# A fused attention and MoE kernel: all attention in native float32, in runs of whole batches between whole blocks of the first MoE product

## The chip, the cores and the metric

The kernel runs on one core of one Trainium2 chip. The metric is device time in microseconds (us), lower is better. PE is TensorE (its weight loads are listed apart as PEld), ACT is ScalarE, DVE is VectorE, POOL is GpSimd, SP is SyncE, which issues the DMAs.

## What is computed

```python
# q, k, v: (8 batches, 12 heads, 448 tokens, 64), float32
scores = scale * q @ k.T - log(448)
attn   = 1 / (1 + exp(-scores))          # a sigmoid, no softmax: no sum over a row
x      = (attn @ v)                      # -> (8*448 tokens, 12*64 = 768)
h      = x @ w_in                        # (3584, 768) @ (768, 2048)
g      = h * clip(h + 3, 0, 6) / 6
out    = g @ w_out                       # (3584, 2048) @ (2048, 768)
```

`w_in` and `w_out` arrive as float64 and are put together on the chip into two float32r parts, high and low.

## The kernel before, in words

**Precision.** A product of float32 accuracy is made in one of two ways. Either both operands are split into a high and a low float32r part and three matmuls are added up (high by high, high by low, low by high), or one matmul is given float32 operands as they are ("native"). A native matmul shows as two records in the trace.

**Attention, native (batches 0 to 2, lines 213 to 259).** Two heads make a pair, 6 pairs a batch. A step takes one chunk of 128 keys for both heads of a pair: two score matmuls on 64 of the 128 rows of the array each (L229), one sigmoid of 128x896 on ACT (L231), two matmuls with v that fill 64 of the 128 columns each (L248). The 64 keys left over (448 = 3 x 128 + 64) of two pairs make one step of quarter tiles, 64x64, the tail (L227, L246). Two pairs are 7 steps, three batches 63 steps. The steps go in groups of two: two steps' scores, then the v products of the group before. Score tiles `sc` have 2 buffers of two PSUM banks. The result of a pair (`pv`) is copied as a high part by ACT (L258) and a low part by DVE (L259) into the blocks `x` that the first MoE product reads.

**Attention, float32r (batches 3 to 7, lines 162 to 211 and 261 to 341).** q, k and v of a pair are split by ACT, DVE and POOL (`prep`), scores take 4 matmuls per chunk (L274, L275) and 3 for the tail (L271), the v products 4 (L331) and 3 (L318). Each chunk has two sigmoids and a subtraction (L279 to L281). After each chunk's scores, 12 matmuls of the first MoE product are put in, up to the end of the last batch: 48 of them and 30 attention matmuls make one pair.

**First MoE product (`moe_in(t)`, L379).** 7 token tiles of 512; each has 16 blocks of 18 matmuls, 288 in all. A block ends in an ACT and a DVE instruction (L383, L384) and a DMA of `g` to DRAM. Its PSUM tile `ph` has 2 buffers. `moe_in(0)` follows the native attention; what is left of the 32 units of w_in (`load_wi`: a DMA, 7 operations on ACT, DVE and POOL, a split) is put together beside it, the first 22 units during the native attention. `moe_in(6)` follows the last attention, and w_out is put together beside it.

**Second MoE product (L543).** 2016 matmuls to the end, beside them reads of `g` and their splits.

**What sets the order.** During batches 0 to 2 and `moe_in(0)` the order on PE, ACT, DVE and POOL is that of the program text; after that only PE's order is. `feed` calls the three parts of a w_in unit (load; join; split) at fixed groups. Each engine works through its own list in order.

Of the kernel before, what the change touches and what calls it, by code (L numbers as in the profile page):

```python
# [20 lines left out]
NST = NC + 1  # L21
# [9 lines left out]
PA = NB * NP  # L31
SB = PA * NST
PEND = 3 * S - 2 * T
LN = 2 * NC
NSN = PA // 2 * (LN + 1)
KB = 3
KM = 12
KU = 14
NSL = 4
NWP = 15  # L40
NWA = 22
NPL = 160
NPP = 224
# [63 lines left out]
def tile_kernel(ctx: ExitStack, tc: tile.TileContext, qk, vP, wi, wo, outT):  # L107
# [33 lines left out]


    zero = att.tile([P, D], F32, tag="x", name="zero", bufs=1)
    nc.gpsimd.memset(zero, 0.0)
    blk = [{n: att.tile([P, P], F32R, tag=f"{n}{u}", name=f"{n}_{u}", bufs=1) for n in ("kbh", "kbl", "vbh", "vbl")} for u in range(2)]

    raw, ops = {}, {}
    qp = []

    def load_native(p):  # L150
        b, hp = divmod(p, NP)
        t = att.tile([P, 2, S], F32, tag=("ka", "ka", "a", "kn")[p % 4], name=f"qkn_{p}", bufs=(2, 2, 1, 1)[p % 4])
        v = att.tile([P, 2 * NC + 1, D], F32, tag=("vv", "vv", "qp0", "qp1")[p % 4], name=f"vn_{p}", bufs=(2, 2, 1, 1)[p % 4])
# [9 lines left out]
    def load(p):  # L163
        b, hp = divmod(p, NP)
        t = att.tile([P, 2, 2, S], F32, tag="qkr", name=f"qkr_{p}", bufs=1)
        v = att.tile([P, 2 * NC + 1, D], F32, tag="vr", name=f"vr_{p}", bufs=1)
        for u in (1, 0):
            for own in halves:
                nc.sync.dma_start(out=t[own, u], in_=qk[b, hp, :, u].rearrange("(j d) s -> d j s", j=2))
        nc.sync.dma_start(out=v, in_=vP[b, hp])  # L170
        raw[p] = t[:, 0], t[:, 1], v

    def prep(p):
        qr, kr, vr = raw.pop(p)
        bk = blk[p % 2]
        qh = att.tile([P, 2, S], F32R, tag="qh", name=f"qh_{p}")
        ql = att.tile([P, 2, S], F32R, tag="ql", name=f"ql_{p}")
        ka = att.tile([P, 2, S], F32R, tag="ka", name=f"ka_{p}")
        nc.vector.tensor_copy(ka, kr)
        for j in range(2):  # L180
            other = halves[1 - j]
            nc.gpsimd.tensor_tensor(  # L182
                out=ka[other, j], in0=kr[other, j], in1=ka.bitcast(F32)[other, j], op=ALU.subtract
            )
        nc.scalar.copy(qh, qr)  # L185
        nc.vector.tensor_tensor(out=ql, in0=qr, in1=qh.bitcast(F32), op=ALU.subtract)  # L186
        vv = att.tile([P, 2, NC, P], F32R, tag="vv", name=f"vv_{p}")
        for j in range(2):
            own, other = halves[j], halves[1 - j]
            vj, vb = vr[:, j * NC : (j + 1) * NC], vr[own, 2 * NC]  # L190
            nc.vector.tensor_copy(vv[:, j, :, own], vj)
            nc.gpsimd.tensor_tensor(  # L192
                out=vv[:, j, :, other], in0=vj, in1=vv.bitcast(F32)[:, j, :, own], op=ALU.subtract
            )
            nc.vector.tensor_copy(bk["vbh"][own, own], vb)
            nc.gpsimd.tensor_tensor(
                out=bk["vbl"][own, own], in0=vb, in1=bk["vbh"].bitcast(F32)[own, own], op=ALU.subtract
            )
        ops[p] = qh, ql, ka, vv

    def prep_block(p):
        qh, ql, ka, _ = ops[p]
        bk = blk[p % 2]
        qp[:] = [att.tile([P, S], F32R, tag=f"qp{u}", name=f"qp{u}_{p}", bufs=1) for u in range(2)]
        for j in range(2):
            own, other = halves[j], halves[1 - j]
            nc.vector.tensor_copy(bk["kbh"][own, own], ka.bitcast(F32)[own, j, NC * P :])
            nc.vector.tensor_copy(bk["kbl"][own, own], ka.bitcast(F32)[other, j, NC * P :])
            nc.vector.tensor_copy(qp[0][own], qh.bitcast(F32)[own, j])
            nc.vector.tensor_copy(qp[1][own], ql.bitcast(F32)[own, j])  # L210

    at = {}

    def native(n):

        m, r = divmod(n, LN + 1)
        return ((2 * m, 2 * m + 1), None) if r == LN else ((2 * m + r // NC,), r % NC)

    def scores_native(n):
        ps, c = native(n)  # L220
        sc = ps_s.tile([P, 2, 512], F32, tag="sc", name=f"scn_{n}")
# [12 lines left out]
    def av_native(n):  # L234
        ps, c = native(n)
        a = at.pop(n)
        for u, p in enumerate(ps):
            v = ops[p][2]
            if c == 0:
                odd = p // 2 % 2  # L240
                pv[p] = (ps_m if odd else ps_a).tile([P, 512], F32, tag="ph" if odd else f"pv{p % 2}", name=f"pv_{p}")
            for j in range(2):
                out = pv[p][halves[j], :S]
                if c is None:
                    rows = halves[j if u == 0 else 1 - j]
                    nc.tensor.matmul(out, v[rows, 2 * NC], a[rows, u], start=False, stop=True)  # L246
                else:
                    nc.tensor.matmul(out, v[:, j * NC + c], a[:, j], start=(c == 0), stop=False)  # L248
        for p in ps if c is None else ():
            b, hp = divmod(p, NP)  # L250
            pt = pv.pop(p)
            for u, (t, c0, q0, n) in enumerate(pieces(b)):
                if u and b == NB - 1:
                    hold(b)
                    nc.vector.tensor_copy(pend[b][:, hp, :n], pt[:, q0 : q0 + n])
                    continue
                xh, xl = (x[:, c0 : c0 + n] for x in block(t, hp))
                nc.scalar.copy(xh, pt[:, q0 : q0 + n])  # L258
                nc.vector.tensor_tensor(out=xl, in0=pt[:, q0 : q0 + n], in1=xh.bitcast(F32), op=ALU.subtract)  # L259

    def scores(s):
        p, c = divmod(s, NST)
        sc = ps_s.tile([P, 2, 512], F32, tag="sc", name=f"sc_{s}")
        last = c == NC
        cs = slice(c * P, min((c + 1) * P, S))
        js = slice(0, 1 if last else 2)
        qh, ql, ka, _ = ops[p]
        if last:
            kbh, kbl = blk[p % 2]["kbh"], blk[p % 2]["kbl"]
            for n, (k_, q_) in enumerate(((kbh, qp[0]), (kbh, qp[1]), (kbl, qp[0]))):  # L270
                nc.tensor.matmul(sc[:, 0, :S], k_, q_, start=(n == 0), stop=(n == 2))  # L271
        else:
            for j in range(2):
                nc.tensor.matmul(sc[:, j, :S], ka[:, j, cs], qh[:, j], start=True, stop=False)  # L274
                nc.tensor.matmul(sc[:, j, :S], ka[:, j, cs], ql[:, j], start=False, stop=True)  # L275
        ah = att.tile([P, 2, S], F32R, tag="ah", name=f"ah_{s}")
        al = att.tile([P, 2, S], F32R, tag="al", name=f"al_{s}")
        a = att.tile([P, 2, S], F32, tag="a", name=f"a_{s}", bufs=1)
        nc.scalar.activation(ah[:, js], sc[:, js, :S], AF.Sigmoid, bias=bias_s, scale=scale)  # L279
        nc.scalar.activation(a[:, js], sc[:, js, :S], AF.Sigmoid, bias=bias_s, scale=scale)  # L280
        nc.vector.tensor_tensor(out=al[:, js], in0=a[:, js], in1=ah.bitcast(F32)[:, js], op=ALU.subtract)  # L281
        at[s] = sc, ah, al

    pv, xf, xb, pend = {}, {}, {}, {}

    def block(t, cc):
# [4 lines left out]
        return xb[t, cc]  # L291

    def hold(b):
        if b not in pend:
            pend[b] = xpl.tile([P, NCC, PEND], F32, tag="pend", name=f"pend_{b}")

    def flush(b):

        t, c0, _, n = pieces(b)[1]
        for cc in range(NCC):  # L300
            xh, xl = (x[:, c0 : c0 + n] for x in block(t, cc))
            x = pend[b][:, cc, :n]
            nc.vector.tensor_copy(xh, x)
# [139 lines left out]
    for s in range(SB, NSTEP + 1):  # L443
# [10 lines left out]
        if s % BS == 1:  # L454
            for _ in moe:
                pass
# [133 lines left out]
```

## Time and profile before

| | |
|---|---|
| median of 3 runs | 1224.88 us (1224.79 to 1225.37) |
| the profiled execution | 1225.24 us, of which the span in the trace 1223.2 us |
| first matmul starts at | 4.15 us |
| native attention (batches 0 to 2) ends at | 116.0 us |
| last attention (batch 7) ends at | 695.1 us |
| second MoE product starts at | 762.4 us |

A row of the trace gives a start or a count, then a duration; what stands behind an arrow (`<-`) ended the idle time before an instruction. The chain is the work that ended last, followed back from the last instruction. Times of merged matmuls include the gaps of their pipeline.

### The profile page before, as it was taken

Reading aid. Unit: us, or ns where it says so; the run is one execution under the profiler, and the core shown is the slowest. Engines: PE = TensorE matmul, PEld = TensorE weight load, DVE = VectorE, ACT = ScalarE, POOL = GpSimd, SP = SyncE. Lnnn points to the kernel's source line nnn. Section 1 sums busy time; section 2 is a strip of 40 time slices with the busy share of each in tenths; the row PEclk is TensorE's granted clock in tenths of the full one; section 3 lists DMA queues with packets and bytes.
Section 4 is the critical chain, followed back from the end, with each engine's and each line's share of the span. In section 5 each row is a group of like instructions: output and inputs, shape, how many; then the busy total and the mean of one; then the engine's idle time right before and its main releaser. Section 6 shows DMA issues by size and latency. Waiting matters only on the chain.

```text
span 1223.2 us, 15074 instructions
## 1 busy us (share of the span) xinstructions
PE 1212.2 (99%) x5508; PEld 960.8 (79%) x5508; DVE 727.2 (59%) x1284; ACT 519.9 (43%) x671; POOL 256.8 (21%) x297
## 2 busy tenths in 40 slices
PE   8999999999999999999999999999999999999998
PEld 2334788888888888888888888888888888888887
DVE  4566868889889888888987598972030303030300
ACT  6776335666666666666656444331010202020200
POOL 3344452333333433434333100000000000000000
PEclk9999999999999999999999999999999999999999
DMA  7644544443334433343432368624040404040000
GB/s 252 195 154 126 162 129 120 118 119 111 105 94 120 118 111 100 99 119 111 118 96 66 93 206 295 232 91 159 26 163 18 164 26 163 27 155 26 26 26 26
DMA packets 62570, 142.68 MB, mean 117 GB/s; under 512 B 8224, under 2 KB 29728, under 8 KB 58912
## 3 DMA queue, kind: packets, MB, share of 16 engines
q1 hardware_dynamic: 62496, 141.72, 36.7%
q8 instruction: 43, 0.70, 0.2%
q14 instruction: 31, 0.25, 0.1%
HBM read 101.32 MB, written 40.37 MB: 116 GB/s over the span
## 4 chain that ended last, share of the span: by engine, by line
PE 95%; DVE 2%; ACT 1%; DMA 1%; issue 1%; POOL 0%; SPq 0%; DVEq 0%; POOLq 0%; ACTq 0%
PE po L543 37%; PE ph L379 36%; PE pv L331 6%; PE scn L229 3%; PE sc L274 3%; PE sc L275 3%; PE pv L248 3%; PE sc L318 1%; PE sc L271 1%; ACT an L231 1%; DMA qkn<-qk 1%; PE scn L227 1%; PE pv L246 0%; DMA qkr<-qk 0%; DVE wiql L60 0%
## 5 line engine op out<-in xcount | busy, mean ns | idle before, releaser
L379 PE MATMUL ph<-x,wi 128*128 128x512 f32 x2016 | 485.7, 391 | 2.4 <-DVE g L384 2.4
L379 PEld LDWEIGHTS ph<-x,wi 128*128 128x128 f32 x2016 | 378.0, 188 | 79.0 <-DVE g L384 4.4
L543 PE MATMUL po<-gh,woh 128*128 128x512 f32 x672 | 261.4, 389 | 0.0
L543 PE MATMUL po<-gl,woh 128*128 128x512 f32 x672 | 261.4, 389 | 0.0
L543 PE MATMUL po<-gh,wol 128*128 128x512 f32 x672 | 261.4, 389 | 0.0
L550 DVE TENSOR_SCALAR o<-po 128x512 f32<-128x512 f32 x42 | 29.0, 690 | 294.1 <-PE po L543 294.1
L503 ACT CAST gh<-gr 128x2048 fp32r<-128x2048 f32 x28 | 53.6, 1914 | 298.1 <-PE po L543 294.0
L281 DVE TENSOR_TENSOR al<-a,ah 128x896 fp32r<-128x896 f32 x120 | 141.3, 1177 | 48.6 <-ACT a L280 47.6
L543 PEld LDWEIGHTS po<-gh,woh 128*128 128x128 f32 x672 | 126.1, 188 | 26.3
L543 PEld LDWEIGHTS po<-gl,woh 128*128 128x128 f32 x672 | 126.1, 188 | 26.2
L543 PEld LDWEIGHTS po<-gh,wol 128*128 128x128 f32 x672 | 126.1, 188 | 26.1
L279 ACT ACTIVATE ah<-sc,bias_s 128x896 fp32r<-128x896 f32 x120 | 110.0, 917 | 73.5 <-PE sc L275 38.0
L182 POOL TENSOR_TENSOR ka<-qkr,ka 64x448 fp32r<-64x448 f32 x60 | 91.7, 1529 | 124.2 <-issue 111.1
L280 ACT ACTIVATE a<-sc,bias_s 128x896 f32<-128x896 f32 x120 | 109.2, 910 | 2.5 <-DVE al L281 1.0
L383 ACT ACTIVATE g<-ph,bias 128x512 f32<-128x512 f32 x112 | 77.1, 688 | 69.0 <-PE ph L379 59.9
L384 DVE SCALAR_TENSOR_TENSOR g<-g,ph 128x512 f32<-128x512 f32 x112 | 76.2, 681 | 18.0 <-ACT g L383 17.7
L504 DVE TENSOR_TENSOR gl<-gr,gh 128x2048 fp32r<-128x2048 f32 x28 | 64.1, 2289 | 29.1 <-ACT gh L503 29.0
L231 ACT ACTIVATE an<-scn,bias_s 128x896 f32<-128x896 f32 x63 | 60.4, 1007 | 23.3 <-PE scn L229 18.4
L274 PE MATMUL sc<-qh,ka 128*128 128x448 f32 x180 | 65.8, 366 | 0.0
L275 PE MATMUL sc<-ql,ka 128*128 128x448 f32 x180 | 65.7, 365 | 0.0
L192 POOL TENSOR_TENSOR vv<-vr,vv 128x192 fp32r<-128x192 f32 x60 | 35.3, 609 | 143.7 <-issue 141.2
L186 DVE TENSOR_TENSOR ql<-qkr,qh 128x896 fp32r<-128x896 f32 x30 | 57.3, 1910 | 5.3 <-ACT qh L185 3.2
(84 smaller groups left out, 1154.4 us busy)
## 6 DMA issues: line engine op xcount, KB each, us to landing
gd<-g SPq DMA_DIRECT2D x112, 256.0 KB, 2.9
gr<-gd SPq DMA_DIRECT2D x28, 1024.0 KB, 5.4
qkr<-qk SPq DMA_DIRECT2D x120, 224.0 KB, 3.9
ws<-wo SPq DMA_DIRECT2D x24, 512.0 KB, 4.9
outT<-o SPq DMA_DIRECT2D x42, 256.0 KB, 2.0
qkn<-qk SPq DMA_DIRECT2D x18, 448.0 KB, 4.6
wiqh<-wi SPq DMA_DIRECT2D x20, 384.0 KB, 3.5
vr<-vP SPq DMA_DIRECT2D x30, 224.0 KB, 2.6
```

Of the source, the lines that this page charges most:

```text
L182: nc.gpsimd.tensor_tensor(out=ka[other, j], in0=kr[other, j], in1=ka.bitcast(F32)[other, j], op=ALU.subtract)
L231: nc.scalar.activation(a, sc[:, :, :S], AF.Sigmoid, bias=bias_s, scale=scale)
L274: nc.tensor.matmul(sc[:, j, :S], ka[:, j, cs], qh[:, j], start=True, stop=False)
L275: nc.tensor.matmul(sc[:, j, :S], ka[:, j, cs], ql[:, j], start=False, stop=True)
L279: nc.scalar.activation(ah[:, js], sc[:, js, :S], AF.Sigmoid, bias=bias_s, scale=scale)
L280: nc.scalar.activation(a[:, js], sc[:, js, :S], AF.Sigmoid, bias=bias_s, scale=scale)
L281: nc.vector.tensor_tensor(out=al[:, js], in0=a[:, js], in1=ah.bitcast(F32)[:, js], op=ALU.subtract)
L331: nc.tensor.matmul(pv[p][j][:, :S], vv[:, j, c, :], a_[:, j], start=(c == 0 and a_ is ah), stop=(c == NC - 1 and a_ is al),)
L379: nc.tensor.matmul(ph, w[:, cc], x, start=(n == 0), stop=(n == 3 * NCC - 1))
L383: i1 = nc.scalar.activation(g, ph, AF.Relu, bias=bias_3, scale=1.0)
L384: i2 = nc.vector.scalar_tensor_tensor(out=g, in0=g, scalar=6.0, in1=ph, op0=ALU.min, op1=ALU.mult)
L543: nc.tensor.matmul(po[t, ec], w[:, fc], x[:, u], start=(fc == 0 and n == 0), stop=(fc == NFC - 1 and n == 2))
```

## The change

All eight batches take the native path; `load` (with its copies), `prep`, `prep_block`, the float32r `scores` and `av` are removed with their splits, second sigmoids and subtractions. Steps go in groups of three (`GS = 3`): the scores of three steps, then the v products of the three steps before. The tail of two pairs is now the fourth of their 7 steps, not the seventh. A batch is a run by itself (21 steps, 7 groups); batches 0 to 2 are one run of 63 steps. Between the runs stand whole `moe_in` blocks with no attention in them: run(0 to 2), `moe_in(0)`, `moe_in(1)`, run(3), `moe_in(2)`, run(4), `moe_in(3)`, run(5), `moe_in(4)`, run(6), `moe_in(5)`, run(7), then `moe_in(6)` as before. The score tiles have 3 buffers (6 PSUM banks), which `ph` of `moe_in(0)` to `moe_in(5)` uses too; `pv` has one buffer for even and one for odd pairs; `moe_in(6)` has 4 buffers. 20 units of w_in, not 22, are put together during the first run, one a group but for one group; the other 12 beside `moe_in(0)`, the last one issued at matmul 238 of 288. The order of all four engines is that of the text up to the end of the last attention.

```diff
-NSL = 4
-NWA = 22
+LC = 2 * NC + 1
+LB = NP // 2 * LC
+GS = 3
+NWA = 20
...
-    ps_m = ph1.enter_context(tc.tile_pool(name="ps_m", bufs=2, space=bass.MemoryType.PSUM, side="right"))
-    att = ph2.enter_context(tc.tile_pool(name="att", bufs=2))
-    ps_s = ph2.enter_context(tc.tile_pool(name="ps_s", bufs=2, space=bass.MemoryType.PSUM))
+    att = ph2.enter_context(tc.tile_pool(name="att", bufs=1))
+    ps_s = ph2.enter_context(tc.tile_pool(name="ps_s", bufs=GS, space=bass.MemoryType.PSUM))
...
+        t = att.tile([P, 2, S], F32, tag="qk", name=f"qk_{p}", bufs=4)
+        v = att.tile([P, 2 * NC + 1, D], F32, tag="v", name=f"v_{p}", bufs=4)
...
+    def step(n):
+        m, r = divmod(n, LC)
+        return ((2 * m, 2 * m + 1), None) if r == NC else ((2 * m + (r > NC),), r % (NC + 1))
...
-        a = att.tile([P, 2, S], F32, tag=("ah", "al")[n % 2], name=f"an_{n}")
+        a = att.tile([P, 2, S], F32, tag="a", name=f"a_{n}", bufs=2 * GS)
...
+        sa = att.tile([P, 4 * w], I32, tag="wis", name=f"wis_{n}", bufs=4)
...
-            ph = (ps_x if t == NT - 1 and fc % 2 else ps_m).tile([P, T], F32, tag="ph", name=f"ph_{t}_{fc}")
+            if t < NT - 1:
+                ph = ps_s.tile([P, 2, T], F32, tag="sc", name=f"ph_{t}_{fc}")[:, 0]
+            else:
+                ph = ps_m.tile([P, T], F32, tag="ph", name=f"ph_{t}_{fc}")
...
+    def attention(first, last, w_in=False):
+        for s in range(first, last, GS):
+            i = (s - first) // GS
+            if w_in:
+                feed(0, i)
+                if s == 0:
+                    load(1)
+                feed(1, i)
+            for n in range(s, s + GS):
+                scores(n)
+            if w_in:
+                feed(2, i)
+            for n in range(s - GS, s):
+                if n >= first:
+                    av(n)
+            for n in range(s, s + GS):
+                m, r = divmod(n, LC)
+                if r in (0, NC) and (p := 2 * m + 2 + (r == NC)) < B * NP:
+                    load(p)
+        for n in range(last - GS, last):
+            av(n)
...
+        attention(0, NB * LB, True)
+        for n, _ in enumerate(moe_in(0)):
+            i, r = divmod(n, KU)
+            if r == 0:
+                for part in range(3):
+                    feed(part, NG0 + i)
+        for n, _ in enumerate(moe_in(1)):
+            if n % (3 * NCC) == 0 and n // (3 * NCC) < NCC:
+                flush(NB - 1, n // (3 * NCC))
+        for b in range(NB, B):
+            attention(b * LB, (b + 1) * LB)
+            if b < B - 1:
+                for _ in moe_in(b - 1):
+                    pass
```

## Rows read from the trace of the kernel before

**Rows 1.** Page, busy time of each engine (share of the span) and its instructions.

```profile
PE 1212.2 (99%) x5508; PEld 960.8 (79%) x5508; DVE 727.2 (59%) x1284; ACT 519.9 (43%) x671; POOL 256.8 (21%) x297
```

**Rows 2.** Waits of PE, all: total us, times, longest us.

```profile
PE scn L229 <- DMA qkn<-qk: 4.2, 1, 4.2
PE ph L379 <- DVE g L384: 2.4, 3, 1.3
PE scn L229 <- ACT an L231: 0.6, 2, 0.3
```

**Rows 3.** Chain in order of time, native attention: start us, us, what; two records a matmul.

```profile
26.30 0.91 PE scn L227 x8
27.22 1.65 PE pv L248 x8
28.87 1.70 PE scn L229 x8
30.57 0.90 PE pv L248 x4
31.48 0.91 PE pv L246 x8
...
40.02 0.95 PE scn L229 x4
...
50.46 0.91 PE scn L227 x8
```

**Rows 4.** Chain, batches 3 to 7 and the MoE products behind them.

```profile
672.57 0.61 PE sc L271 x3
...
684.45 0.81 PE pv L331 x4
...
689.63 0.61 PE sc L271 x3
...
695.09 67.36 PE ph L379 x297
762.45 456.97 PE po L543 x2016
```

**Rows 5.** Chain at the start of the native attention.

```profile
4.15 5.79 PE scn L229 x16
9.94 1.65 PE pv L248 x8
11.60 1.70 PE scn L229 x8
13.30 1.65 PE pv L248 x8
14.96 0.91 PE scn L227 x8
```

**Rows 6.** Timeline of PE, end of the native attention: start us, us, what.

```profile
116.01 8.46 PE L379 MATMUL ph<-x,wi 128*128 128x512 f32 x36
125.05 49.74 PE L379 MATMUL ph<-x,wi 128*128 128x512 f32 x216 [0.58 <-DVE g L384]
```

**Rows 7.** Chain, two places in the native attention where PE waits for a sigmoid.

```profile
59.25 0.91 ACT an L231
...
60.21 1.92 PE scn L229 x8
...
83.37 0.56 ACT wis L58
83.92 0.91 ACT an L231
...
84.87 1.92 PE scn L229 x8
```

**Rows 8.** ACT by line and shape, 4 to 116 us: count, busy us, mean ns, idle before.

```profile
L231 ACT ACTIVATE an<-scn,bias_s 128x896 f32<-128x896 f32 x63 | 60.4, 1007 | 23.3 <-PE scn L229 18.4 <-PE scn L227 4.6
```

**Rows 9.** Stretch 60 to 90: PE, PEld, DVE, ACT, POOL busy us, granted clock, DMA.

```profile
60.00:90.00 30.00, 29.50 (x156) 9.20 (x156) 20.49 (x42) 23.82 (x39) 11.62 (x12) 1.00 0.46 145
```

More of the change, by code (lines that the diff above doesn't have):

```diff
@@ L20 @@
 NC = S // P
-NST = NC + 1
 NP = H // 2
@@ L30 @@
 NB = 3
-PA = NB * NP
-SB = PA * NST
 PEND = 3 * S - 2 * T
[L34 to L37, printed above, removed]
+LC = 2 * NC + 1
+LB = NP // 2 * LC
+GS = 3
 KU = 14
-NSL = 4
-NWP = 15
-NWA = 22
-NPL = 160
-NPP = 224
+NWA = 20
 NWU = 1.4
@@ L140, in tile_kernel, with load @@
     nc.scalar.activation(warm, bias_s, AF.Sigmoid)
[L143 to L150, printed above, removed]
+    ops, at, pv, xb, pend = {}, {}, {}, {}, {}
+    def load(p):
         b, hp = divmod(p, NP)
-        t = att.tile([P, 2, S], F32, tag=("ka", "ka", "a", "kn")[p % 4], name=f"qkn_{p}", bufs=(2, 2, 1, 1)[p % 4])
-        v = att.tile([P, 2 * NC + 1, D], F32, tag=("vv", "vv", "qp0", "qp1")[p % 4], name=f"vn_{p}", bufs=(2, 2, 1, 1)[p % 4])
+        t = att.tile([P, 2, S], F32, tag="qk", name=f"qk_{p}", bufs=4)
+        v = att.tile([P, 2 * NC + 1, D], F32, tag="v", name=f"v_{p}", bufs=4)
         nc.sync.dma_start(out=t, in_=qk[b, hp])
@@ L161, in load_native @@
         ops[p] = t[:, 0], t[:, 1], v
[L163 to L221, printed above, removed]
+    def step(n):
+        m, r = divmod(n, LC)
+        return ((2 * m, 2 * m + 1), None) if r == NC else ((2 * m + (r > NC),), r % (NC + 1))
+    def scores(n):
+        ps, c = step(n)
+        sc = ps_s.tile([P, 2, 512], F32, tag="sc", name=f"sc_{n}")
@@ L229, in scores_native @@
                     nc.tensor.matmul(sc[:, j, :S], k[halves[j], c * P : (c + 1) * P], q[halves[j]], start=True, stop=True)
-        a = att.tile([P, 2, S], F32, tag=("ah", "al")[n % 2], name=f"an_{n}")
+        a = att.tile([P, 2, S], F32, tag="a", name=f"a_{n}", bufs=2 * GS)
         nc.scalar.activation(a, sc[:, :, :S], AF.Sigmoid, bias=bias_s, scale=scale)
         at[n] = a
[L234 to L282, printed above, removed]
@@ L284, in tile_kernel @@
-    pv, xf, xb, pend = {}, {}, {}, {}
     def block(t, cc):
@@ L291, in block, with flush @@
         return xb[t, cc]
[L293 to L297, printed above, removed]
+    def flush(b, cc):
         t, c0, _, n = pieces(b)[1]
[L300 to L303, printed above, removed]
-            nc.vector.tensor_tensor(out=xl, in0=x, in1=xh.bitcast(F32), op=ALU.subtract)
-    def av(s):
-        p, c = divmod(s, NST)
-        b, hp = divmod(p, NP)
-        last = c == NC
-        vv = ops[p][3]
-        if c == 0:
-            pv[p] = [ps_a.tile([P, 512], F32, tag=f"pv{u}", name=f"pv{u}_{p}") for u in range(2)]
-        sc, ah, al = at.pop(s)
-        if last:
-            vbh, vbl = blk[p % 2]["vbh"], blk[p % 2]["vbl"]
-            out = sc[:, 1, :S]
-            for n, (v_, a_) in enumerate(((vbh, ah), (vbl, ah), (vbh, al))):
-                nc.tensor.matmul(out, v_, a_[:, 0], start=(n == 0), stop=(n == 2))
-            x = xf.pop(p)
-            (t, c0, q0, n), *rest = pieces(b)
-            nc.vector.tensor_tensor(out=x[:, :n], in0=out[:, :n], in1=x[:, :n], op=ALU.add)
-            xh, xl = (x_[:, c0 : c0 + n] for x_ in block(t, hp))
-            nc.vector.tensor_copy(xh, x[:, :n])
-            nc.gpsimd.tensor_tensor(out=xl, in0=x[:, :n], in1=xh.bitcast(F32), op=ALU.subtract)
-            for _, _, q0, n in rest:
-                hold(b)
-                nc.vector.tensor_tensor(out=pend[b][:, hp, :n], in0=out[:, q0 : q0 + n], in1=x[:, q0 : q0 + n], op=ALU.add)
-            return
-        for a_ in (ah, al):
-            for j in range(2):
-                nc.tensor.matmul(
-                    pv[p][j][:, :S], vv[:, j, c, :], a_[:, j],
-                    start=(c == 0 and a_ is ah), stop=(c == NC - 1 and a_ is al),
-                )
-        if c == NC - 1:
-            pt = pv.pop(p)
-            x = xf[p] = att.tile([P, S], F32, tag="x", name=f"x_{p}", bufs=1)
-            for j in range(2):
-                own, other = halves[j], halves[1 - j]
-                nc.scalar.copy(x[own], pt[j][other, :S])
-                nc.vector.tensor_tensor(out=x[own], in0=pt[j][own, :S], in1=x[own], op=ALU.add)
@@ new lines, in flush, with av @@
+        xh, xl = (x[:, c0 : c0 + n] for x in block(t, cc))
+        x = pend[b][:, cc, :n]
+        nc.vector.tensor_copy(xh, x)
+        nc.vector.tensor_tensor(out=xl, in0=x, in1=xh.bitcast(F32), op=ALU.subtract)
+    def av(n):
+        ps, c = step(n)
+        a = at.pop(n)
+        for u, p in enumerate(ps):
+            v = ops[p][2]
+            if p not in pv:
+                pv[p] = ps_a.tile([P, 512], F32, tag=f"pv{p % 2}", name=f"pv_{p}")
+            for j in range(2):
+                out = pv[p][halves[j], :S]
+                if c is None:
+                    rows = halves[j if u == 0 else 1 - j]
+                    nc.tensor.matmul(out, v[rows, 2 * NC], a[rows, u], start=(u == 1), stop=(u == 0))
+                else:
+                    nc.tensor.matmul(
+                        out, v[:, j * NC + c], a[:, j],
+                        start=(p % 2 == 0 and c == 0), stop=(p % 2 == 1 and c == NC - 1),
+                    )
+        p = ps[0]
+        if c is None or (p % 2 and c == NC - 1):
+            b, hp = divmod(p, NP)
+            pt = pv[p]
+            for u, (t, c0, q0, w) in enumerate(pieces(b)):
+                if u and b == NB - 1:
+                    if b not in pend:
+                        pend[b] = xpl.tile([P, NCC, PEND], F32, tag="pend", name=f"pend_{b}")
+                    nc.vector.tensor_copy(pend[b][:, hp, :w], pt[:, q0 : q0 + w])
+                    continue
+                xh, xl = (x[:, c0 : c0 + w] for x in block(t, hp))
+                nc.scalar.copy(xh, pt[:, q0 : q0 + w])
+                nc.vector.tensor_tensor(out=xl, in0=pt[:, q0 : q0 + w], in1=xh.bitcast(F32), op=ALU.subtract)
@@ L355, in load_wi @@
         hi, lo = (w_[fc][:, cs].rearrange("p c f -> p (c f)") for w_ in (wih, wil))
-        own = n % NSL if n < NWP else n % (NSL - 1)
-        if own == 2:
-            sa = att.tile([P, 4 * w], I32, tag="qkr", name=f"wis_{n}", bufs=1)
-            st, ab = sa[:, : 2 * w], sa[:, 2 * w :]
-        elif own == 3:
-            sa = xpl.tile([P, 4 * w], I32, tag="pend", name=f"wis_{n}")
-            st, ab = sa[:, : 2 * w], sa[:, 2 * w :]
-        else:
-            st, ab = (att.tile([P, 2 * w], I32, tag=tag, name=f"wi{tag}_{n}") for tag in ("qh", "ql"))
+        sa = att.tile([P, 4 * w], I32, tag="wis", name=f"wis_{n}", bufs=4)
+        st, ab = sa[:, : 2 * w], sa[:, 2 * w :]
         st, ab = st.rearrange("p (n t) -> p n t", t=2), ab.bitcast(F32)
@@ L373, in moe_in @@
         for fc in range(NFC):
-            ph = (ps_x if t == NT - 1 and fc % 2 else ps_m).tile([P, T], F32, tag="ph", name=f"ph_{t}_{fc}")
+            if t < NT - 1:
+                ph = ps_s.tile([P, 2, T], F32, tag="sc", name=f"ph_{t}_{fc}")[:, 0]
+            else:
+                ph = ps_m.tile([P, T], F32, tag="ph", name=f"ph_{t}_{fc}")
             n = 0
@@ L386, in moe_in @@
             nc.sync.dma_start(out=gd[t][fc // GF][:, fc % GF], in_=g)
-    NU = (NSN + 1) // 2
-    first = [n * NU // NWA for n in range(NWA)]
-    first += [NU - 1 + int((n - NWA) * NWU) for n in range(NWA, 2 * NFC)]
+    NG0 = NB * LB // GS
+    ways = []
+    for n in range(2 * NFC):
+        i = n * NG0 // NWA
+        k = NG0 + 1 + int((n - NWA) * NWU)
+        ways.append((i, i + 2, i + 3) if n < NWA else (k - 3, k, k + 1))
     way = {}
     def feed(part, i):
-        for n in range(2 * NFC):
-            if first[n] + ((0, 2, 3) if n < NWA else (0, 3, 4))[part] == i:
+        for n, parts in enumerate(ways):
+            if parts[part] == i:
                 if part == 0:
@@ L400, in feed @@
                 next(way[n], None)
-    with tc.manual_schedule(
-        engines={mybir.EngineType.PE, mybir.EngineType.Activation, mybir.EngineType.DVE, mybir.EngineType.Pool}
-    ):
-        load_native(0)
-        for i in range(NU + 1):
-            feed(0, i)
-            if i == 0:
-                load_native(1)
-                for u in range(2):
-                    for t in blk[u].values():
-                        for j in range(2):
-                            nc.gpsimd.tensor_copy(t[halves[j], halves[1 - j]], zero[halves[j]])
-            feed(1, i)
-            steps = [n for n in (2 * i, 2 * i + 1) if n < NSN]
-            for n in steps:
-                scores_native(n)
-            feed(2, i)
-            for n in (2 * i - 2, 2 * i - 1):
-                if 0 <= n < NSN:
-                    av_native(n)
-            for n in steps:
-                m, r = divmod(n, LN + 1)
-                if r in (0, NC) and (p := 2 * m + 2 + r // NC) < PA:
-                    load_native(p)
-        moe = moe_in(0)
-        for n in range(NFC * 3 * NCC - KM):
+    def attention(first, last, w_in=False):
[19 more added lines that the diff above has]
+            av(n)
+    engines = {mybir.EngineType.PE, mybir.EngineType.Activation, mybir.EngineType.DVE, mybir.EngineType.Pool}
+    with tc.manual_schedule(engines=engines):
+        load(0)
+        attention(0, NB * LB, True)
+        for n, _ in enumerate(moe_in(0)):
             i, r = divmod(n, KU)
@@ L430, in tile_kernel @@
                 for part in range(3):
-                    feed(part, NU + 1 + i)
-            if n == NPL:
-                load(PA)
-            if n == NPP:
-                prep(PA)
-            next(moe)
-    ctx.enter_context(tc.manual_schedule(engines={mybir.EngineType.PE}))
-    load(PA + 1)
-    quota = 0.0
-    NSTEP = B * NP * NST
-    BS = NP * NST
-    for s in range(SB, NSTEP + 1):
-        p, c = divmod(s, NST)
-        b = p // NP
-        if s < NSTEP:
-            scores(s)
-            if c == 1:
-                prep_block(p)
-            if c == 2 and p + 1 < B * NP:
-                prep(p + 1)
-            if c == 3 and p + 2 < B * NP:
-                load(p + 2)
-        if s % BS == 1:
-            for _ in moe:
-                pass
-            flush(b - 1)
-            moe = moe_in(b - 2)
-        quota += KM
-        for _ in range(KB if c == 0 else KM):
-            if quota >= 1:
-                next(moe, None)
-                quota -= 1
-        if s > SB:
-            av(s - 1)
-        while quota >= 1:
-            next(moe, None)
-            quota -= 1
-    for _ in moe:
-        pass
+                    feed(part, NG0 + i)
[7 more added lines that the diff above has]
+                    pass
+    ctx.enter_context(tc.manual_schedule(engines={mybir.EngineType.PE}))
     ph2.close()
@@ L474, in tile_kernel @@
     stp = ctx.enter_context(tc.tile_pool(name="stp", bufs=3, reuse_waits="tile"))
-    ps_x = ph1.enter_context(tc.tile_pool(name="ps_x", bufs=2, space=bass.MemoryType.PSUM, side="right"))
+    ps_m = ph1.enter_context(tc.tile_pool(name="ps_m", bufs=4, space=bass.MemoryType.PSUM, side="right"))
     ps_o = ctx.enter_context(tc.tile_pool(name="ps_o", bufs=4, space=bass.MemoryType.PSUM, reuse_waits="tile"))
```

## The prediction, made before the changed kernel was run

> **What bounds the kernel now.** I read the busy shares first, then PE's waits, then the chain. PE is busy for 1212.2 of 1223.2 us [rows 1], and its waits sum to 7.2 us: the first load, 2.4 us for DVE's `g`, 0.6 us for sigmoids [rows 2]. In the attention and MoE stages almost every piece of the chain is PE's [rows 3, 4]. So PE's own work sets the time, and all that the change takes off ACT, DVE and POOL (splits of q, k and v, second sigmoids, subtractions) is worth nothing by itself: PE never waits for it in batches 3 to 7. The question is only how long PE takes for the same attention in the other form, and whether new waits arise where MoE matmuls no longer stand between dependent steps.
>
> **Price of a native step.** Two steps' scores take 1.70 us, one 0.95; two steps' v products 1.65, one 0.90 [rows 3]. So a step more costs 0.75 us on either side, and entering the group costs 0.20 (scores) or 0.15 (v products) beside it. A tail takes 0.91 [rows 3]: 0.75 and 0.16 for the change of tile. Test: from the tail at 26.30 to that at 50.46 are 14 steps in 7 groups with 2 tails, 24.16 us [rows 3]; the terms give 28 x 0.75 + 7 x 0.35 + 4 x 0.16 = 24.09. Four pairs in 24.16 are 6.04 us a pair.
>
> The Trainium skill (TensorEngine Tiling (Array Packing), Key Properties) says that a change of tiling mode drains the engine; the trace agrees, with 0.15 to 0.20 us a change [rows 3]. That rule speaks against the change, since float32r attention has one mode for all its matmuls; were those changes free, the sum below would come out about 17 us lower for batches 3 to 7. The Trainium skill (FP8 and Floating Point Precision, TensorE Precision Notes) says that true float32 takes four passes through the array; if the two heads of a step did not run side by side, a half step would by that be an estimated 1.5 us and the kernel some 140 us slower than before, but the 0.75 us for both heads [rows 3] show that they do.
>
> **Price of a float32r pair.** From one tail's scores at 672.57 to the next at 689.63 are 17.06 us [rows 4], with 48 MoE matmuls in them. A MoE matmul is 67.36 / 297 = 0.2268 us [rows 4], 48 are 10.89, so attention is 6.17 us a pair, 37.0 a batch. (Four v matmuls take 0.81 and three tail ones 0.61 [rows 4]: 6 x 0.81 + 2 x 0.61 = 6.08; the other 0.09 is what the mixing costs.)
>
> **Batches 3 to 7 after the change.** A batch is 21 steps: 42 half steps x 0.75 = 31.5. It has 7 groups of scores and 7 of v products; the first two of scores and the last two of v products touch, so 6 entries of each: 6 x 0.35 = 2.1. The three tails stand first, in the middle and last in their groups. At an end of a group a tail costs one change more, 0.16; in the middle two, 0.36 among scores and 0.31 among v products: 0.68 + 0.63 = 1.31. Going back to MoE: the first 36 MoE matmuls behind the native stage take 8.46 us [rows 6] against 36 x 0.2268 = 8.16, so 0.30. At the start of a run the second group of scores meets the sigmoids: the first sigmoid starts about 1.1 us after its scores do, three of them at 0.96 us each (0.91 to 1.01 [rows 7, 8]) end 4.0 us after the start, where the sixth step's scores could begin at 2.45 + 1.5 = 3.95; I take 0.15 us. Nothing of this wait is in the trace of before. Its bounds: 0, and the whole excess of the kernel's start, 14.96 - 4.15 = 10.81 us [rows 5] against 10 x 0.75 + 2 x 0.35 = 8.2, that is 2.6 us. I stay near the low end because the two stalls in the warm stage cost only (0.31 idle and 1.92 - 1.70 [rows 7]) 0.53 us each. Sum: 31.5 + 2.1 + 1.31 + 0.30 + 0.15 = 35.4 us, against 37.0. Five batches: **8.4 us less** (177 against 185).
>
> **First run.** 126 x 0.75 + 20 x 0.35 + 3 x 1.31 = 105.4 us, and the same 2.6 us at the start: 108.0 us, against 116.01 - 4.15 = 111.9 [rows 5, 6]. **3.8 us less**, of which about 1.1 are the two stalls. They came from ACT: at 60.21 and 84.87 PE waited for a sigmoid that stood behind copies of a finished pair or behind the first operation of a w_in unit [rows 7]. With three score buffers the scores of the third step in a group wait for a sigmoid that ended over 2 us before, so I take no stall. ACT has 23.8 us in 30 [rows 9] and would have the same work in 4 us less: still under PE's.
>
> **MoE blocks.** The 2.4 us of waits [rows 2] come with 2 buffers: DVE's `g` stood behind w_in and q, k, v splits. A third buffer gives it one block more, 18 x 0.2268 = 4.1 us, against a longest wait of 1.3 [rows 2], and the splits of q, k and v are gone: **2.4 us less**. Bounds 0 and 2.4. What is left of w_in there grows from 10 units to 12; the last is issued at matmul 238 and wanted at 279, 41 x 0.2268 = 9.3 us later, so it costs nothing; if the units fell behind by more, PE would wait for the rest.
>
> **Edits at nothing.** `pv` with one buffer for each parity: the next pair of a parity starts its v products three steps later (2.3 us and a group of scores at least), which covers the copies (under 1.5 us). Results of the last pair of a run are wanted at the 16th matmul of the MoE block, 3.4 us in. Loads for the next pairs are issued 7 steps ahead (11.8 us); SP's queue then has fewer bytes than before, since q and k are no longer loaded twice. The 4 w_in slots turn over in four groups, 19 us, so a load may wait on SP for POOL's split of the unit four before, and the pair loads behind it too, by about 1 us of 11.8. From `moe_in(6)` on nothing changes: 528 us from 695.09 [rows 4] to the end.
>
> **Sum.** 8.4 + 3.8 + 2.4 = 14.6 us. The profiled execution took 1225.24 us, so 1210.6; the median of the runs lies 0.36 below it: **1210.3 us**. A second way: 4.15 + 108.0 + 0.3 + 1728 x 0.2268 + 177 = 681.4 us for the start of `moe_in(6)`, which was at 695.09 + 9 x 0.2268 = 697.1: 15.7 us less, 1209.2. The ways differ by 1.1 us that lie between 125 and 190 us, where PE's rows are a little longer than their steady price [rows 6].
>
> **Rivals.**
> - *A: groups of three save nothing*, because the extra of a group belongs to its steps (the next weights come late, say). Then a pair is 6.04 as now, a batch 36.24 + 0.45, five save 1.8 us; the first run saves only its stalls, 1.1; MoE 2.4. That is 5.3 us: 1219.6. For it: no group of three is in the trace. Against it: 0.95 and 1.70 [rows 3] leave only 0.75 for the second step.
> - *B: the waits stay.* ACT in order behind w_in stalls the first run as now, DVE's `g` is late as now: 11.1 us, 1213.8. For it: the same work in a shorter run [rows 9].
> - *C, the slower side: a wait on the sigmoid in every group.* Before, MoE matmuls lay between scores and v products in batches 3 to 7; now there is nothing else for PE to do. If each of the 21 + 35 = 56 groups waited the 0.53 us of the two stalls [rows 7], that is 29.7 us: 1240.0. It decides from 14.6 / 56 = 0.26 us a group. It needs ACT to take longer than PE for a group: three sigmoids of 1.007 us [rows 8] and one share of copies, some 3.7 us, and with w_in 4.2 (112 x 23.8 / 30 over 21 groups [rows 9]), against 4.85 of PE. That is against it.
> - *D: each of the five runs starts as slowly as the first one* (2.6 us and not 0.15): 12.2 us back, 1222.5. Against it: PE comes straight from MoE matmuls, while at 4.15 us it comes from idling.
>
> **Chances.** Forecast 0.64, A 0.13, B 0.12, C 0.06, D 0.05. The forecast's own range is 1207 (the second way, less up to 2 us if the first run's start shrinks) to 1212.5. It and B hold 0.76; to leave out no more than 0.2 the range must take in A: 1207 to 1219.7. A measurement of this kernel can tell about 0.2%, 2.4 us, from no change: faster by more than that are the forecast, A and B, 0.89; D lies at that edge, 0.05 for no difference; C 0.06 slower.
>
> **What would show it.** Right: scores of three steps in one piece of about 2.45 us and v products of 2.40 in the chain; a batch's run of 35 to 36 us; first run over at about 112 us; `moe_in(6)` starting near 682; no PE wait for `g`. A: three steps' scores at 2.55 or more. B: waits of PE on L383/L384's successors or on sigmoids, 1 us and 2.4 us in sum. C: PE's waits for ACT in the tens. D: the first group of a run over 3.5 us long. The prediction is wrong if a run takes over 37 us, or if what follows 682 us is no longer 528 us long.

## The result, and the profile after

The changed kernel takes 1212.07 us (median of 4 runs, 1211.90 to 1214.08), the kernel before beside it 1224.87: a ratio of 0.9898, 95% interval 0.9881 to 0.9916. That is 12.8 us less; 14.6 were forecast.

The page of the changed kernel, busy time of each engine, answers to [rows 1]:

```profile
PE 1200.8 (99%) x5568; PEld 852.4 (70%) x5568; DVE 366.3 (30%) x606; ACT 372.1 (31%) x500; POOL 64.6 (5%) x70
```

DVE lost half of its work, POOL three quarters, ACT 148 us, and the time follows PE alone, which has 11.4 us less to do. Its waits, against [rows 2]:

```profile
PE sc L163 <- DMA qk<-qk: 4.3, 1, 4.3
PE ph L246 <- DVE x L212: 1.3, 1, 1.3
```

The waits for `g` (2.4 us) and for sigmoids (0.6) are gone, and one of 1.3 us is new. The chain in order of time (start us, us, what), first run, against [rows 3, 5]:

```profile
4.27 4.52 PE sc L163 x12
...
11.40 2.40 PE pv L196 x12
13.81 2.46 PE sc L163 x12
...
18.83 0.95 PE sc L163 x4
19.78 0.91 PE sc L161 x8
20.70 0.95 PE sc L163 x4
21.65 2.41 PE pv L196 x12
...
112.37 17.70 PE ph L246 x77
```

Three steps' scores take 2.46 us and their v products 2.40: the price of 0.75 a half step and of 0.20 and 0.15 an entry, extrapolated from groups of one and two, holds for three (2.45 and 2.40). A tail in the middle of its group is at 18.83 to 21.65: 0.95, 0.91, 0.95. The timeline of PE around a batch's run and its MoE block (start us, us, what):

```profile
243.10 2.60 PE L163 MATMUL sc<-qk 64*128 64x448 f32 x12
245.63 0.98 PE L161 MATMUL sc<-qk 64*64 64x448 f32 x8
246.54 1.77 PE L163 MATMUL sc<-qk 64*128 64x448 f32 x8
248.25 2.48 PE L196 MATMUL pv<-a,v 128*64 128x448 f32 x12
...
276.12 2.48 PE L196 MATMUL pv<-a,v 128*64 128x448 f32 x12
278.52 65.57 PE L246 MATMUL ph<-x,wi 128*128 128x512 f32 x288
344.02 2.60 PE L163 MATMUL sc<-qk 64*128 64x448 f32 x12
```

The run lasts 278.52 - 243.10 = 35.42 us, and the block 344.02 - 278.52 = 65.50, which is 0.18 over 288 x 0.2268. The seam at the last MoE block and the second product, in the chain, against the last two of [rows 4]:

```profile
682.34 0.54 ACT x L211
...
682.90 0.64 DVE x L212
...
683.58 65.58 PE ph L246 x288
749.16 457.25 PE po L385 x2016
```

PE ends its last v products at 682.3 and does nothing for 1.29 us, until DVE has written the low part of the last pair, though the first matmuls of the block don't read that pair.

### The profile page after: what moved, and what is told of

Same layout as the page of the kernel before. It is cut to its first block, busy times and chain, and to the rows that moved or that the text cites. A ratio compares the mean times of both kernels' runs of the same rounds, so it can differ in the third digit from the quotient of the medians.

```text
span 1210.1 us, 13738 instructions
## 1 busy us (share of the span) xinstructions
PE 1200.8 (99%) x5568; PEld 852.4 (70%) x5568; DVE 366.3 (30%) x606; ACT 372.1 (31%) x500; POOL 64.6 (5%) x70
## 4 chain that ended last, share of the span: by engine, by line
PE 99%; DMA 0%; DVE 0%; ACT 0%; issue 0%
PE ph L246 38%; PE po L385 38%; PE sc L163 10%; PE pv L196 10%; PE pv L194 2%; PE sc L161 2%; DMA qk<-qk 0%; DVE o L392 0%; DVE x L212 0%; ACT x L211 0%
## 5 line engine op out<-in xcount | busy, mean ns | idle before, releaser
L246 PE MATMUL ph<-x,wi 128*128 128x512 f32 x2016 | 458.8, 389 | 1.3 <-DVE x L212 1.3
L165 ACT ACTIVATE a<-sc,bias_s 128x896 f32<-128x896 f32 x168 | 157.1, 1007 | 52.4 <-PE sc L163 52.1
L163 PE MATMUL sc<-qk 64*128 64x448 f32 x576 | 127.9, 568 | 4.3 <-DMA qk<-qk 4.3
L196 PE MATMUL pv<-a,v 128*64 128x448 f32 x576 | 122.4, 550 | 0.0
L163 PEld LDWEIGHTS sc<-qk 64*128 64x128 f32 x576 | 50.6, 189 | 77.7 <-issue 37.3
L196 PEld LDWEIGHTS pv<-a,v 128*64 128x64 f32 x576 | 35.6, 136 | 80.4 <-issue 77.3
L212 DVE TENSOR_TENSOR x<-pv,x 128x448 fp32r<-128x448 f32 (+6 forms) x78 | 32.7, 420 | 195.0 <-ACT x L211 195.0
L211 ACT CAST x<-pv 128x448 fp32r<-128x448 f32 (+6 forms) x78 | 28.8, 369 | 37.3 <-DVE x L212 14.4
L60 POOL TENSOR_TENSOR wis<-wis 128x384 f32<-128x384 f32 x32 | 32.3, 1010 | 95.6 <-DVE wis L57 95.6
L66 POOL TENSOR_TENSOR wi<-wis,wi 128x384 fp32r<-128x384 f32 x32 | 32.5, 1024 | 7.9 <-ACT wi L65 7.7
```

The costliest lines, as they stand in the source:

```text
L60: nc.gpsimd.tensor_tensor(out=a, in0=a, in1=b, op=ALU.add)
L66: nc.gpsimd.tensor_tensor(out=lo, in0=a, in1=hi.bitcast(F32), op=ALU.subtract)
L163: nc.tensor.matmul(sc[:, j, :S], k[halves[j], c * P : (c + 1) * P], q[halves[j]], start=True, stop=True)
L196: nc.tensor.matmul(out, v[:, j * NC + c], a[:, j], start=(p % 2 == 0 and c == 0), stop=(p % 2 == 1 and c == NC - 1),)
L212: nc.vector.tensor_tensor(out=xl, in0=pt[:, q0 : q0 + w], in1=xh.bitcast(F32), op=ALU.subtract)
L246: nc.tensor.matmul(ph, w[:, cc], x, start=(n == 0), stop=(n == 3 * NCC - 1))
```

## The experiments

The theory: PE's own time sets the kernel's; a half step of native attention costs 0.75 us and each change of tile 0.15 to 0.20; so what matters is how often PE changes tile, and that no wait takes the place of the MoE matmuls that lay between. Rival A says that groups save nothing, rival C that the sigmoids bind a group once nothing lies between.

**1. The new wait.** The PSUM pool of the last block, `ps_m`, opens only when the attention's pools close, so its first tile waits for all of them.

```diff
-    ps_m = ...tile_pool(name="ps_m", bufs=4, space=bass.MemoryType.PSUM, side="right"))
+    ps_m = ...tile_pool(name="ps_m", bufs=4, space=bass.MemoryType.PSUM, side="right", reuse_waits="tile"))
```

> The PSUM pool of the last block of the first MoE product hands over its banks tile by tile instead of all at once. Theory: the 1.29 us that PE waits at the first matmul of that block is the wait of the whole pool for the last copy of the last pair, so it goes: some 1.3 us less than the changed kernel, about 1210.8 us, and the block starts at 682.3 instead of 683.6. Rival: the matmuls really need that copy; then the wait only moves to the 13th to 16th matmul and the time stays at 1212.1.

Measured: 1214.16 us (1211.18 to 1215.96; before 1225.66 beside it), ratio 0.9903 (0.9885 to 0.9921). PE's waits:

```profile
PE sc L163 <- DMA qk<-qk: 4.0, 1, 4.0
PE po L385 <- DVE gl L346: 2.4, 1, 2.4
```

The wait at the seam is gone, so it was the pool's; the block starts at 681.9, 1.7 us earlier (0.3 of them because the first load landed earlier). But more than that is lost 70 us later. The end of the chain, and the timeline of PE there:

```profile
753.16 2.29 DVE gl L346
...
755.50 453.15 PE po L385 x1991
```

```profile
755.50 0.79 PE L385 MATMUL po<-gl,woh 128*128 128x512 f32 x1 [2.35 <-DVE gl L346]
756.10 0.63 PE L385 MATMUL po<-gh,wol 128*128 128x512 f32 x1
756.52 0.63 PE L385 MATMUL po<-gh,woh 128*128 128x512 f32 x1
```

After 25 of its matmuls the second product waits for the low part of the third group of `g`, which DVE comes to late behind splits of w_out. Behind the wait the granted clock is 0.50 from 755.5 to 758.7 us, the 1.2 GHz level, and matmuls start 0.43 us apart, not 0.23; so the last 1991 take 453.15 us, 1.6 more than 1991 x 0.2268. The wait of 2.35 us costs 3.9. In the profiled execution of the changed kernel the same instruction of DVE held the same matmul up by only 0.14 us:

```profile
754.44 0.39 PE L385 MATMUL po<-gh,woh 128*128 128x512 f32 x1
754.81 0.50 PE L385 MATMUL po<-gl,woh 128*128 128x512 f32 x1
```

Experiments 8 to 10 come back to it.

**2 to 4. Groups, buffers, whole blocks, taken back one by one.** Experiment 2 goes back to groups of two and keeps three score buffers and six for sigmoids:

```diff
-GS = 3
+GS = 2
+NSC = 3
...
-    ps_s = ph2.enter_context(tc.tile_pool(name="ps_s", bufs=GS, ...))
+    ps_s = ph2.enter_context(tc.tile_pool(name="ps_s", bufs=NSC, ...))
...
-            for n in range(s, s + GS):
+            for n in range(s, min(s + GS, last)):
```

> Groups of two steps in the changed kernel, three score buffers and six sigmoid buffers kept. Theory (0.20 us for each entry into scores, 0.15 for each into v products, 0.16 to 0.20 for each change to or from a tail, 0.75 a half step): a batch's run 36.0 us instead of 35.4, the first run 110.8 instead of 108.1, in all 5.8 us more: 1217.8. Rival (the extra belongs to the steps, groups save nothing): run lengths and time unchanged, 1212.1. If the first run stalls on sigmoids as before the change, up to 1 us more.

Experiment 3 is the same with `NSC = 2`:

> As the kernel with groups of two, but with two score buffers, which the MoE blocks use too, as before the change. Theory: the first run gets back about 1 us of waits for sigmoids, the start of each of five runs about 0.5 us, the MoE block beside w_in up to 2.4 us of waits for DVE: 1219 to 1223. Rival: the third buffer is worth nothing, 1217.8, and PE's waits stay as they are in the kernel with groups of two and three buffers.

Experiment 4 mixes attention and MoE again, as before the change but native; results that the MoE block in hand still needs room for go through `pend`:

```diff
+NSC = 2
+MIX = 13
...
             for n in range(s, min(s + GS, last)):
                 scores(n)
+            for _ in range(MIX if moe else 0):
+                next(moe, None)
             for n in range(s - GS, s):
                 if n >= first:
                     av(n)
+            for _ in range(MIX if moe else 0):
+                next(moe, None)
...
-            attention(b * LB, (b + 1) * LB)
-            if b < B - 1:
-                for _ in moe_in(b - 1):
-                    pass
+            for cc in range(NCC):
+                flush(b - 1, cc)
+            moe = moe_in(b - 2)
+            attention(b * LB, (b + 1) * LB, moe=moe)
+            for _ in moe:
+                pass
```

> Native attention in batches 3 to 7, but mixed with MoE matmuls as before the change: groups of two, two score buffers, two MoE buffers, 13 MoE matmuls between the scores and the v products of a group and 13 after them. Theory: each group of two pays 0.20 + 0.18 + 0.15 + 0.18 = 0.71 us for changes of tile instead of 0.35, 11 groups a batch, five batches: 19 us more than the kernel with groups of two and two buffers, near 1240 us, so slower than the kernel before the change: native attention pays only in whole blocks. Rival: mixing costs as little as it did with float32r (0.09 us a pair, 2.7 us in all): 1222 to 1225.

All three ran beside the same runs of before (1225.66 us):

| | median, us | ratio (95%) | span of the profile, us |
|---|---|---|---|
| 2: groups of two, 3 buffers | 1218.92 | 0.9946 (0.9931 to 0.9961) | 1215.7 |
| 3: groups of two, 2 buffers | 1224.53 | 0.9992 (0.9983 to 1.0001) | 1222.2 |
| 4: the same, mixed | 1246.26 | 1.017 (1.0155 to 1.0185) | 1245.2 |

The timeline of PE in experiment 2, MoE blocks of batches 3 and 4:

```profile
281.39 65.57 PE L247 MATMUL ph<-x,wi 128*128 128x512 f32 x288
383.01 65.58 PE L247 MATMUL ph<-x,wi 128*128 128x512 f32 x288
```

From block to block are 101.62 us, less 65.50 of MoE is a run of 36.12 (36.0 expected; 35.42 in groups of three). Its first run ends at 114.5 (112.3). Rival A falls: the extra belongs to the group. PE's waits in experiment 3:

```profile
PE sc L164 <- DMA qk<-qk: 4.2, 1, 4.2
PE sc L164 <- DVE g L252: 2.7, 5, 0.5
PE sc L162 <- ACT a L166: 2.4, 6, 0.4
PE ph L247 <- DVE x L213: 1.3, 1, 1.3
```

and its timeline at the start of a run:

```profile
348.42 1.02 PE L164 MATMUL sc<-qk 64*128 64x448 f32 x4
349.99 1.77 PE L164 MATMUL sc<-qk 64*128 64x448 f32 x8 [0.55 <-DVE g L252]
352.18 0.98 PE L162 MATMUL sc<-qk 64*64 64x448 f32 x8 [0.42 <-ACT a L166]
```

The third buffer is worth 6.5 us of span (5.6 by the medians; experiment 2's runs spread over 3 us), more than was expected: 1224.5 lies above 1219 to 1223. At the start of each of five runs the second step waits for the last `g` of the MoE block, then a step for a sigmoid (0.97 us idle; from block to block a run is 1.2 us longer). Two expectations were wrong. The first run ends only 0.2 us later (114.7), not 1 us. And no `ph` matmul beside w_in waits for `g` any more, with two buffers either. Before the change there were three such waits [rows 2], one of 0.58 us [rows 6] and these (timeline of PE before the change):

```profile
176.10 8.46 PE L379 MATMUL ph<-x,wi 128*128 128x512 f32 x36 [0.49 <-DVE g L384]
186.71 3.00 PE L379 MATMUL ph<-x,wi 128*128 128x512 f32 x12 [1.34 <-DVE g L384]
```

Ahead of `g` on DVE stood float32r splits in these two (L207 to L210; L281 and L186), 1.83 us in all, and those went with the change. In the one of 0.58 us it was the joining of w_in (L59 to L65), which is still there. So the third buffer isn't what removes the waits; why the one of 0.58 us is gone is not shown. The timeline of PE in experiment 4, inside a batch:

```profile
413.56 3.24 PE L246 MATMUL ph<-x,wi 128*128 128x512 f32 x13
416.73 0.97 PE L199 MATMUL pv<-a,v 128*64 128x448 f32 x4
```

From 413.56 to 416.73, 13 MoE matmuls take 3.17 us where 13 x 0.2268 are 2.95: going into them costs 0.22, twice a group. At the second product PE waits 2.4 us for `gl`, and behind that wait 1991 matmuls take 453.19 us, 1.6 too many, as in experiment 1. In all the span is 23 us longer than that of experiment 3, and the kernel is 1.7% slower than before the change. Native attention by itself, put where the float32r attention was, loses; here it wins only in whole blocks, and in groups of two the whole blocks win only with the third buffer (experiment 3 can't be told from the kernel before).

**5 and 6. Does ACT bind a group?** In the runs of batches 3 to 7 each step gets one more sigmoid on ACT, of 128 or of 448 columns:

```diff
         at[n] = a
+        if n >= NB * LB:
+            ...
+            nc.scalar.activation(e[:, 0], sc[:, 0, :S], AF.Sigmoid, bias=bias_s, scale=scale)
```

> In the runs of batches 3 to 7 each step has a further sigmoid of 128x128 on ACT, behind its own, whose result nobody reads. Theory: PE sets the time, ACT has room in a group of three steps (three sigmoids of 1.007 us and about 0.6 us of copies against 5.06 us a group); some 0.35 us a step more, 1.05 a group, is 4.7 us: runs stay at 35.4 us, the time at 1212. Rival (the sigmoids already bind each group): 35 groups times 1.05, 37 us more, 1249.

> The same with a further sigmoid of 128x448 (0.64 us) a step. Theory: ACT then has 5.6 us of work in a group against 5.06 of PE and becomes the bound by some 0.5 us a group: a run of 39 us, 17 us more in all, about 1229. If ACT's delay went to PE whole, 35 times 1.9, 67 us more, 1279; if ACT had more room than I think, no change.

Measured: 1214.24 us with the small one and 1218.92 with the large one (before 1224.79 beside them; ratios 0.9914, 0.9894 to 0.9934, and 0.9952, 0.9936 to 0.9968). So 2.2 more than the changed kernel where 0 was expected, 6.8 where 17 was. PE's waits with the large one, those with a sigmoid at their end:

```profile
PE sc L164 <- ACT extra L172: 4.2, 10, 0.4
```

and its timeline of ACT at the start of a run:

```profile
346.78 1.01 ACT L166 ACTIVATE a<-sc,bias_s 128x896 f32<-128x896 f32 x1 [0.28 <-PE sc L164]
347.69 0.63 ACT L172 ACTIVATE extra<-sc,bias_s 128x448 f32<-128x448 f32 x1
348.20 1.01 ACT L166 ACTIVATE a<-sc,bias_s 128x896 f32<-128x896 f32 x1
```

Back to back, a sigmoid of 1.01 us starts the next instruction after 0.91, the extra one of 0.63 after 0.51. I had added durations; by these starts a group has 3 x 1.42 + 0.6 = 4.9 us of ACT against 5.06 of PE, so even the large one fits. What it costs lies at the starts: there are ten waits, two for each of five runs, and a run grows by 1.3 us, with the small one by 0.5 (from block to block 102.25 and 101.45 against 100.93, means of three). Rival C falls inside the runs, where ACT has room for half as much work again; at the start of a run it has none, because the first six steps' scores follow each other with no v products between them.

**7 and 8. Fewer changes of tile.** Groups of three and four by turns, so that a tail always opens a group of four; with the edit of experiment 1. In experiment 8 the split of `g` is also placed earlier (`GSL`). `groups` gives the steps m to m+2 and m+3 to m+6 of each two pairs.

```diff
-        for s in range(first, last, GS):
-            i = (s - first) // GS
+        before = ()
+        for i, (s, end) in enumerate(groups(first, last)):
...
-GSL = 56
+GSL = 44
```

> Groups of three and four by turns, so that the tail is always the first step of a group of four, with PSUM banks handed over one by one as in the first experiment. Theory: for two pairs PE changes mode 6 times, 1.02 us, where groups of three take 3.85 us for three times two pairs: a run of 34.6 us instead of 35.4, the first run 106 instead of 108.1, 6 us less than the changed kernel in all and 1.3 us for the wait at the last MoE block, so that the second MoE product starts near 742 us instead of 749.2: near 1205 us, or 1207.5 where the second product then waits for its operand as it did in the first experiment. Rival: four scores in a row wait for sigmoids with three score buffers, then the run stays at 35.4 us or grows.

> As the kernel with groups of three and four, and the split of a group of g for the second product is placed 44 instead of 56 matmuls behind the start of its block of the first one. Theory: the 2.4 us that PE waited for that split in the first experiment come from DVE reaching it late behind the w_out splits; 12 matmuls (2.7 us) earlier it is in time: about 1204.5 us, and the runs of this kernel lie within 1 us of each other. Rival: the operand's read itself is late, then the wait stays or moves to ACT and the time is that of the kernel before it.

Measured beside the same runs of before (1224.79): 1212.02 us (1211.04 to 1212.97), ratio 0.9899 (0.9882 to 0.9915), and 1208.34 (1208.16 to 1208.53), ratio 0.9866 (0.9851 to 0.9881). PE's waits in experiment 7, which keeps the late split:

```profile
PE sc L163 <- DMA qk<-qk: 4.1, 1, 4.1
PE po L389 <- DVE gl L350: 1.7, 1, 1.7
PE sc L163 <- ACT a L165: 1.0, 2, 0.5
PE sc L161 <- DMA qk<-qk: 0.7, 1, 0.7
PE ph L246 <- DVE g L251: 0.5, 1, 0.5
```

The timeline of PE in experiment 8, a wait in the first run and the MoE blocks of batches 3 and 4:

```profile
70.52 1.02 PE L163 MATMUL sc<-qk 64*128 64x448 f32 x4 [0.54 <-ACT a L165]
...
278.91 65.58 PE L246 MATMUL ph<-x,wi 128*128 128x512 f32 x288
379.13 65.58 PE L246 MATMUL ph<-x,wi 128*128 128x512 f32 x288
```

A run is 379.13 - 278.91 - 65.50 = 34.72 us, as expected (34.6). The first run didn't shorten: it lasts 108.6 us, not 106, for with fewer, longer groups beside w_in two waits for sigmoids are back (1.1 us idle, each group 0.8 longer), and one wait for `g` of 0.4 (0.5 in experiment 7), with three buffers and no float32r splits. So 3.5 of the hoped-for 6 us come, in the five later runs, and the time is 3.8 us over the 1204.5 expected. And the split of `g` decides the rest: with it at its old place PE waits 1.7 us in the profile and the runs spread over 1.9 us; 12 matmuls earlier they lie within 0.4.

**9 and 10. The split alone, and a control.** Experiment 9 is experiment 1 with `GSL = 44`; experiment 10 is the changed kernel unaltered, beside it.

> The changed kernel (groups of three) with PSUM banks handed over one by one, as in the first experiment, and the split of g for the second product placed 12 matmuls earlier. Theory: both waits at the seams go (1.29 us at the last MoE block, up to 2.4 us at the second product in some executions): 1210.5 us, 1.5 us under the changed kernel run beside it, all its runs within 1 us. Rival: the gain of the last kernel with groups of three and four came from its groups alone; then this one stays at 1212 to 1214 with a spread of 2 us or more.

> The changed kernel once more, unaltered, on the same chip as the experiment beside it. Theory: 1212 us, with single executions some 2 us longer, in which PE waits at the second product for the split of g. Rival: the execution of 1214 us was chance of the chip alone; then all lie within 0.5 us.

Measured beside the same runs of before (1224.72): 1210.44 us (1210.24 to 1211.05), ratio 0.9882 (0.9865 to 0.9898), and for the control 1212.68 (1212.14 to 1213.24), ratio 0.9898 (0.9884 to 0.9913). The two changes are worth 2.2 us (1.5 expected), and the ranges don't meet: they help without the new groups. PE's only wait in experiment 9:

```profile
PE sc L163 <- DMA qk<-qk: 4.0, 1, 4.0
```

The end of the chain in the control:

```profile
752.75 2.30 DVE gl L346
...
755.09 451.61 PE po L385 x1991
```

In this execution of the control, one of its faster, the split of `g` held the second product up by 0.28 us (0.14 in the first profile of the same kernel). Its runs fall into two pairs, near 1212.2 and 1213.2. A longer wait at the same place in the slower pair would explain that, but no slower run has a profile, so it is not shown.

The fastest version is experiment 8: 1.34% under the kernel before, 4 us under the changed one.

## Why the prediction was right

The time (1212.07) lies in the range, and the forecast mechanism is the one measured. Term by term:

- **What bounds.** That work off ACT, DVE and POOL is worth nothing by itself is borne out: DVE halved, and the gain is PE's. Experiment 4 is the strongest sign: the same work is off the three engines there, and the kernel is slower than before.
- **First run**: 108.0 us forecast, 112.37 - 4.27 = 108.1 measured. That it is so close is luck: the start costs 2.1 us above the steady price, not 2.6 (11.40 - 4.27 = 7.13 against 2.45 + 0.91 + 1.70 = 5.06), and the rest takes 106.0, not 105.4, for the most part for the reason given next.
- **A batch's run**: 35.4 forecast with the entry into MoE in it; 35.42 + 0.18 = 35.6 measured. Small errors nearly cancel, which is luck too: the entry is 0.18, not 0.30; the second group of scores doesn't wait for sigmoids at all (0.91 and 1.71 from start to start), where I took 0.15, and only the first scores, entered from MoE, take 0.07 more (2.53 against 2.46); but I took the two adjacent groups at either end of a run for one entry saved, where a tail stands at that very seam and the tile changes anyway, 0.20 + 0.15.
- **The MoE waits**: 2.4 us gone as forecast, for half the reason given. The step "A third buffer gives it one block more" isn't needed (experiment 3 has two buffers and no such wait), nor does it protect (experiments 7 and 8 have three and a wait). The splits that went explain 1.83 us; for 0.58 the cause stays open. The third buffer earns its 6.5 us elsewhere, at the starts of the runs, where I had priced it at nothing.
- **Sum to the last MoE block**: leaving out its new wait, 13.55 + 1.29 = 14.8 us earlier (697.13 to 683.58), against 14.9 forecast (the 14.6 hold the entry into this block, 0.30, which comes behind its start).
- **What failed** is one of the edits at nothing: "From `moe_in(6)` on nothing changes". The first matmul of that block waits 1.29 us for a pool that didn't exist before, and the second product is 0.3 us longer (457.25 against 456.97): its 26th matmul starts 0.14 us late behind the split of `g`, and the next ones a little later still. I read PE's waits and not how close the operand had come. With the entry into the block (0.26) that makes 14.8 - 1.3 - 0.3 - 0.3 = 13.0 of the 13.1 us of span. One run of the changed kernel is 2 us longer (1214.08); that a longer wait at the same place did it is likely by experiment 1, but not shown.
- **Rival C** was rightly put low but with too little room: I added ACT's durations (1.007 us) where the starts are 0.91 apart.
- **The drain of the Trainium skill** (TensorEngine Tiling (Array Packing), Key Properties: changing the mode drains the engine) fits the runs: every change costs PE time, 0.15 to 0.22 us each. No run shows whether the drain itself or the weight loads make up that time.

What each part is worth, in spans of the profiles: native and mixed instead of float32r and mixed, 1223.2 to 1245.2, 22 us lost; whole blocks, to 1222.2, 23 won (4 of either are experiment 4's wait for `gl` and the clock behind it); the third buffer, to 1215.7, 6.5; groups of three, to 1210.1, 5.6.

## What to carry to other kernels

Where one engine is busy all the time, price a rewrite in its instructions and in its changes of mode, each from rows that differ by one step; then the order in which work of different modes is grouped can be worth more than the choice of the mode. Count entries to a group by writing the sequence out, seams included. And before an edit downstream is costed at nothing, look how late its operands come: one that arrives just in time shows no wait and gives back what was gained upstream.

## What was not expected of the hardware

- The scores of the kernel's first three steps take 4.52 us, 1.5 each, twice the 0.75 of later ones, while the granted clock in that stretch (4.2 to 8.7 us) reads 1.00, the 2.4 GHz level; PE had been idle until then. The later runs, which follow MoE matmuls at once, start at full pace. The column alone would not have shown it.
- An ACT instruction lets the next one start some 0.1 us before its own end in the profile (1.01 against 0.91 us), so durations overstate a full queue by a tenth.
- After a wait of 2.35 us on PE (experiment 1) and one of 2.41 (experiment 4) the granted clock went to 0.50, the 1.2 GHz level, for some 3 us, which cost 1.6 us more; after one of 1.75 us in experiment 7 it stayed at 1.00. A wait can cost more than the idle time that the waits' table shows.
